# A long convolution and a feed-forward layer: earlier loads, a transform stage in 64-by-64 parts, products on a third engine, and a new deal of the tasks

## The chip, the cores and the metric

The kernel runs on one core of a Trainium2 chip. A core has five engines, each with its own queue of instructions that it issues in order: TensorE (PE; its weight loads are shown apart as PEld), VectorE (DVE), ScalarE (ACT), GpSimd (POOL) and SyncE (SP), which here issues nearly all DMA transfers. The metric is the time of one execution on the device, in microseconds (us).

## The reference, cut to what matters

```
x = A_u                                            # (1, 2048, 640)
mod = (silu(c) @ w_mod).reshape(1, 6, 1, -1)       # sa, ca, ga, sb, cb, gb
h = layernorm(x) * (1 + ca) + sa
  # A_ref(h): a convolution over the whole length L = 2048, per channel
  dt = exp(log_dt); A = -exp(log_A_real) + 1j * A_imag; C = (C_real + 1j * C_imag) * dt
  P = exp((A * dt)[:, :, None] * arange(L));  K = 2 * einsum("dn,dnl->dl", C, P).real
  y = irfft(rfft(h, 2 * L) * rfft(K, 2 * L))[:L]
x = x + ga * (y + h * D_skip)
h = layernorm(x) * (1 + cb) + sb
x = x + gb * ((silu(h @ w1) * (h @ w3)) @ w2)      # 640 -> 1728 -> 640
```

There are 640 channels, 128 states per channel, 2048 tokens.

## The kernel before, in words

The program has two parts. The **convolution** works in five blocks of 128 channels, counted 0 to 4 here. A token has the number 64 t1 + 16 q + j (t1 below 32, q below 4, j below 16), and the transforms of length 4096 are split in two stages along such numbers. For each block:

- *Generation* of the convolution's own kernel K, in eight chunks of 16 channels (`gen_chunk`): GpSimd makes phases (`ph<-p,p`) and sizes (`yy<-e,e`), ScalarE five sines (`tr<-ph`), VectorE five products (`yy<-yy,tr`, `xx<-tr,xx`), PE sums over the states in 32 matmuls (`kps<-yy,xx`), ScalarE copies to `ks`, VectorE adds the skip term.
- *Tokens*: the block's columns are normalised (`hn`, `hb`), written to DRAM (`hs`) and read back as `xb`.
- *First transform stage* (`first_tasks`): eight groups for the tokens (`ps<-wk,xb`), eight for K (`ps<-wk,ks`). A group is 8 matmuls of 64 x 128 tiles into one PSUM bank, and one copy by ScalarE or VectorE to `sp`, which holds both spectra's halves. In fp32 each matmul shows as two rows. A K group takes columns of all chunks, so the stage needs all eight chunks of its block.
- *Second stage and product* (`spectra_tasks`), eight spectra w.0 to w.7: PE makes `fh` (tokens) and `fk` (K), ScalarE holds `fh` in `hq`, VectorE multiplies with four instructions: `fp<-fk,hq`, `fk<-fk,hq`, and two sums into `fp`.
- *Inverse*: one per pair of spectra, z.0 to z.3 (`fz<-fp,wz`), whose two banks ScalarE or VectorE copies to `zt`; SP stores them in DRAM (`zd`).

Then **the last inverse stage** (`inverse`, matmuls `iy`, table `wd`, 1 MB, half of it zeros) reads `zd` back (`low<-zd`), adds the tokens x2 and gathers the second layernorm's sums. Its first rows (`ir0`, `ir1`) already run at the end of the convolution with the first four blocks' channels; the last block's channels follow when its stores are done, after eight `awake` matmuls that keep PE busy. The **feed-forward part** has 14 tiles of weights; each is split in a high part (ScalarE, `wh`) and a low part (GpSimd or VectorE, `wl`). Raw tiles `wr` (and `w2r`) have two buffers each, so that a third load waits for the split of the first. The first two tiles, 0 and 13, are loaded and split at the end of the convolution: tasks fw (load), fa (high part), fs (low part).

What sets the order: `run` lists all tasks of the convolution in a `Plan`, each with its engine and the tasks that it needs. The text ORDER is a list of task numbers; `Plan.run` issues the tasks in just this order (a letter a, d or p at a number picks ScalarE, VectorE or GpSimd where there is a choice), and `InOrder` ties each instruction to the one before on its engine. So every instruction of the convolution has the line of that helper, L147, in the profile. The task `change`, after the last generation chunk, closes the pools of the generation (`gw`, `tbl`, `gp`) and opens those of the feed-forward part. In it stand the loads of the first tokens and of `wd`; fw0, fw1 and the loads of the first rows (iz0, iz1) need it. These loads have one more condition, `behind`: they also wait for the last PE instruction ahead of them in the text:

```
nc.sync.behind = nc.tensor.prev
self.load_x2(0)
nc.sync.dma_start(self.wd, self.t_wd)
nc.sync.behind = None
```

Of the kernel before, what the change touches and what calls it, by code (L numbers as in the profile page):

```python
# [25 lines left out]
NB = 5  # L26
# [4 lines left out]
WA = 2  # L31
SIGN = -2 ** 31
# [11 lines left out]
284 294 285 298 352 148 458 299 445 149 0 582 698d 446 300 447 442 353d 592 324 699 443 450 328 325d 461 583d 336 459 460 329d  # L44
577 584 334 444 451 337a 585 301 972p 335a 700d 586 326 462 452 302 330 434 578d 327a 331a 354 448 467 593a 332 437p 579 438
468 439 580 333a 435 856 594 338 355a 453 449 436 358 463 581 595 851 464 475 440 364 454 469 465 455 339d 596 466 470 356 456
476 479 457 362 471 357 477 484 480 472 363 359 492 481 485 360 473 482 365 495 496 361 366 478 379 487 493 380 486 494 367
483 501 497 373 701 488 852a 375 502 857d 489 374 509 498 381 853 587 490 858 499 510 854 513 1399 859 390 704p 504 705 706
391 860 503 855 511 491 474 518 500 376 514 702 505 515 526 377 506 382 378 507 512 383 588a 407 519 527 384 520 528 408 385
861 589 516 703 508 530 590 517 521 591 368 529 707 388a 386a 522 389 543 531 387 536 523 532 537 1400d 369a 392 544 597 524  # L50
862a 545 525 393 1140 535 546 371a 394 533 1401 398 547 372 395 534 1402 1130 560 539 396 553 413 552 397 538 708 414 1403 370
399 540 548 863 564 400 549 561 864 565 554 709 865 598 541 566 569 710 542 401 550 599d 608 1131a 562 555 602 563 570 609a
1132 711p 606 973 712 571 713 604 1133 603d 714 1134 612 607d 1141d 600 601d 866 605a 974p 1142 567 610 613d 1246p 1404 1143
409 611d 551 572 670 568 1144 715 410 867a 636 573 411 574 732 556 719 1135 637 868 557 575 412 671 736 869 630 718 558 1405d
870 720 664 716 721 653 726 717 631 1409 1406 665 647 733 654 725 1407 871 648 734 741 1136a 415 681 724 735 1408 742 616 559
416 737 1414 1137 617a 743 738 417 682 1138 739 418 1139 687 722 744 1410a 620 727 880 723 1411 1125 688 728 749 881a 618 1412
740 576 1413 1415d 621a 729 766 753 876 619a 754 745 1126a 872 1416 750 1417 746 752 873d 1418 877a 1127 624 770 767 760 755
614 1128 768 625a 775 1129 628 615a 758 751 776 626 629a 769 759 622 627d 771 975 882 756 623d 772 761 402 883a 777 773 976
978d 730 778 979 419 774 980 403a 779 747 977 404 757 405d 632 420a 731 748 406 762 783 981 421 649 633 634 780 650 800 787
638 635 781 788 782 651 422a 763 639 789 423 652 655 784 764 640 790 884 656 801 641 878 885a 802 657 792 874 879a 785 658 765  # L60
786 875a 793 642 795 804 803 794 886 645a 643d 791 646 666 810 644 887a 817 1145 796 805 910 667 806 811 797 911 809 921 668
807 820 669 821 938 818 922 812 808 904 819 798 813 822 672 799 905 826 834 823 827 814 673 939 927 828 824 835 674 815 659
# [35 lines left out]
def shape_tables():  # L98
# [22 lines left out]
    wd = np.zeros((2, 32, 2, NJ, 2, 2, 32))  # L121
# [64 lines left out]
class K:  # L186
# [385 lines left out]
    def inverse_half(self, i, ps, tag, bufs):  # L572

        u, h = 2 + i // 2, i % 2
        if h == 0:
            self.zu = self.inverse_load(4608 + u % 2 * 2560, 2 * u, 2, 0, D)
# [1206 lines left out]
```

## Time and profile before

| | us |
|---|---|
| median of 3 runs | 968.23 (967.66 to 969.07) |
| the profiled execution | 967.95 |
| its span in the trace | 966.0 |
| PE busy in the span | 856.0 (89%) |
| VectorE busy | 713.6 (74%) |
| ScalarE busy | 518.4 (54%) |
| GpSimd busy | 336.2 (35%) |
| first matmul of the last inverse stage on the last block | 388.43 after the span's start |

The profiled execution is one among those timed; the span is what the trace shows from the first to the last instruction, and the remaining 1.95 us lie around it. A row such as `fk<-sp,wb 128*64 128x128 f32 x16` names output and inputs, the tile of PE, partitions by elements of the output, type and count. A bracket at a row's end is idle time of that engine before the row, and what ended it.

### The profile page before, as it was taken

What the parts mean: (1) busy time and instruction counts of PE and PEld (TensorE: products, weight loads), DVE (VectorE), ACT (ScalarE), POOL (GpSimd) and SP (SyncE); (2) the same over time, 40 slices, a digit from 0 to 9 for tenths busy, and PEclk for the clock granted to TensorE, in tenths of its full rate; (3) what the DMA queues carried; (4) which work ended last, traced back from release to release, by engine and by line L of the source; (5) the groups of instructions that cost most, each with busy time, mean ns of one, the idle gap of its engine ahead of it and who ended that gap; (6) DMA issues with size and microseconds to landing.
All of it is one profiled execution on the core that took longest, in us unless ns stands there. A gap on an engine that the chain in (4) does not pass through costs nothing.

```text
span 966.0 us, 20403 instructions
## 1 busy us (share of the span) xinstructions
PE 856.0 (89%) x8145; PEld 681.2 (71%) x8145; DVE 713.6 (74%) x1292; ACT 518.4 (54%) x874; POOL 336.2 (35%) x345
## 2 busy tenths in 40 slices
PE   2164867899999996899999999999999999999997
PEld 1033755787878772577787778888888888888875
DVE  7888899999999974565666486566468777765763
ACT  5889879979888840442343244344234444445331
POOL 2799898599999730100000000000113222300000
PEclk9597889999999997999999999999999999999999
DMA  9955426624040277875545263233031111123242
GB/s 245 253 172 209 106 61 168 162 70 111 25 111 25 69 224 230 200 202 150 158 121 137 82 157 103 82 85 106 28 82 55 55 55 55 42 82 92 86 150 82
DMA packets 124934, 113.20 MB, mean 117 GB/s; under 512 B 12328, under 2 KB 107048, under 8 KB 123432
## 3 DMA queue, kind: packets, MB, share of 16 engines
q1 hardware_dynamic: 124072, 110.99, 42.4%
q8 instruction: 64, 1.05, 0.5%
q10 hardware_dynamic: 768, 0.92, 0.4%
q14 instruction: 30, 0.25, 0.1%
HBM read 90.91 MB, written 20.97 MB: 116 GB/s over the span
## 4 chain that ended last, share of the span: by engine, by line
PE 57%; DVE 2%; DMA 2%; ACT 1%; issue 0%; SPq 0%; DVEq 0%; ACTq 0%
PE p L789 17%; PE acc L1036 16%; PE gu L999 7%; PE gu L1001 6%; PE gu L1000 6%; DMA wq<-in_w 1%; PE iy L562 1%; PE awake L147 1%; PE q L789 1%; PE tp L613 1%; PE fz L147 1%; DMA zd<-zt 0%; PE acc L147 0%; DVE w2l L988 0%; PE iy L147 0%; DVE wq L983 0%
## 5 line engine op out<-in xcount | busy, mean ns | idle before, releaser
L999 PE MATMUL gu<-xh,wh 128*128 128x512 f32 x270 | 106.0, 398 | 0.9 <-ACT xh L581 0.7
L1001 PE MATMUL gu<-xh,wl 128*128 128x512 f32 x270 | 105.4, 390 | 0.0
L1000 PE MATMUL gu<-xl,wh 128*128 128x512 f32 x270 | 105.2, 390 | 0.0
L789 PE MATMUL p<-x,wch 128*128 128x512 f32 x312 | 92.6, 390 | 0.0
L808 POOL TENSOR_TENSOR ws<-wp 128x256 f32<-128x256 f32 x13 | 9.6, 740 | 230.9 <-DVE x L582 116.0
L147 POOL TENSOR_TENSOR yy<-e,e 128x512 f32<-128x512 f32 x80 | 86.0, 1089 | 4.8 <-PE kps L147 3.6
L147 POOL TENSOR_TENSOR ph<-p,p 128x1024 int32<-128x1024 int32 x40 | 78.0, 1953 | 16.4 <-ACT tr L147 16.0
L147 DVE TENSOR_TENSOR yy<-yy,tr 128x512 f32<-128x512 f32 (+1 forms) x80 | 75.3, 946 | 1.6 <-POOL yy L147 1.2
L147 PE MATMUL kps<-yy,xx 128*32 128x64 f32 x2560 | 51.3, 235 | 23.2 <-DVE xx L147 12.9
L693 ACT ACTIVATE wh<-wr 128x640 fp32r<-128x640 f32 x51 | 34.9, 731 | 68.2 <-PE gu L1000 61.1
L147 PEld LDWEIGHTS kps<-yy,xx 128*32 128x32 f32 x2560 | 45.0, 117 | 34.0 <-issue 16.2
L789 PEld LDWEIGHTS p<-x,wch 128*128 128x128 f32 x312 | 58.3, 188 | 12.5 <-ACT s L824 0.4
L999 PEld LDWEIGHTS gu<-xh,wh 128*128 128x128 f32 x270 | 50.6, 188 | 16.8 <-issue 2.1
L1001 PEld LDWEIGHTS gu<-xh,wl 128*128 128x128 f32 x270 | 50.7, 188 | 11.3 <-DVE wl L702 0.4
L1000 PEld LDWEIGHTS gu<-xl,wh 128*128 128x128 f32 x270 | 50.7, 188 | 10.2 <-DVE xl L582 0.2
L789 PE MATMUL p<-x,wcl 128*128 128x512 f32 x156 | 57.0, 389 | 0.0
L147 ACT ACTIVATE tr<-ph,hpi 128x512 f32<-128x512 f32 x80 | 54.5, 689 | 3.0 <-DVE yy L147 2.1
L147 DVE TENSOR_TENSOR xx<-tr,xx 128x512 f32<-128x512 f32 x80 | 54.4, 682 | 1.7 <-ACT tr L147 1.5
L705 POOL MEMSET w2l<- 64x640 f32 x1 | 0.6, 632 | 157.0 <-PE acc L1036 157.0
L826 DVE TENSOR_TENSOR s<-p,s 128x512 f32<-128x512 f32 x52 | 34.8, 683 | 26.8 <-ACT s L824 22.8
L147 PE MATMUL ps<-wk,xb 128*64 128x128 f32 x640 | 46.8, 297 | 5.3 <-DVE hb L147 2.5
L1014 DVE TENSOR_TENSOR a<-a,gu 128x512 f32<-128x512 f32 x26 | 17.9, 687 | 45.5 <-PE gu L1001 45.4
(368 smaller groups left out, 2299.3 us busy)
## 6 DMA issues: line engine op xcount, KB each, us to landing
wr<-in_w SPq DMA_DIRECT2D x52, 320.0 KB, 3.6
zd<-zt SPq DMA_DIRECT2D x39, 256.0 KB, 2.7
w2r<-in_w SPq DMA_DIRECT2D x26, 320.0 KB, 3.0
wp<-in_w SPq DMA_DIRECT2D x26, 320.0 KB, 3.6
wq<-in_w SPq DMA_DIRECT2D x26, 320.0 KB, 3.2
low<-zd SPq DMA_DIRECT2D x48, 160.0 KB, 5.4
xs<-in_x SPq DMA_DIRECT2D x16, 320.0 KB, 9.8
hs<-hb SPq DMA_DIRECT2D x20, 256.0 KB, 2.7
```

The source lines that it names most:

```text
L147: self.prev = self.k.order(f(*a, **kw), self.prev)
L562: mm = nc.tensor.matmul(py[p][c:c + 32, :n], self.wd[r:r + 64, j0 + j + p, q // 2, c % 64:c % 64 + 32], z[q // 2][r:r + 64, j + p, o:o + n ...
L613: nc.tensor.transpose(pt[:, j * P:(j + 1) * P], xn[:, j, k * P:(k + 1) * P], self.ident)
L693: self.nc.scalar.activation(wh[:, i], raw[:, i], AF.Copy)
L789: nc.tensor.matmul(to, t[:, o], y[:, k], start=start and k == i == 0, stop=stop and (k, i) == (n - 1, 2), skip_group_check=True)
L808: G.tensor_tensor(s[0], a21, a22, op=ALU.add)
L826: add = lambda o, bk, s: V.tensor_tensor(o, bk, s, op=ALU.add)
L999: nc.tensor.matmul(pg, wh[:, k, :], xh[:, k, :], start=(k == 0), stop=False)
L1000: nc.tensor.matmul(pg, wh[:, k, :], xl[:, k, :], start=False, stop=False)
L1001: nc.tensor.matmul(pg, wl[:, k, :], xh[:, k, :], start=False, stop=(k == KT - 1))
L1014: nc.vector.tensor_mul(a, a, gu[1])
L1036: nc.tensor.matmul(acc[k], *two(a, w), start=(m == 0 and i == 0), stop=(m == 12 and i == 2))
```

## The change

**Memory.** Two pools are opened at the start and live to the end: `wrp` (two `wr`, two `w2r`; during the convolution they hold the tables pB, pS, al and mag) and `xp` (one tile of 3584 columns: first the tables of the odd blocks' sizes, then the first tokens with `wd`, then a part of the pair data of the feed-forward part). `wd` is stored without its zeros, 0.5 MB instead of 1 MB. The first rows' loads iz0 go to `xb`. `low` shrinks from 11264 to 7680 columns. Small early tiles lie in slices of the tile for layernorm sums.

**Loads.** fx (first tokens and `wd`), fw0, fw1 and iz0 no longer need `change`, and `behind` is gone there. They stand earlier in SP's order: fx among the stores of block 2, fw0 behind them, fw1 among the stores of block 3.

**K's first stage** in blocks 1 to 4 (`kernel_tasks`): four groups instead of eight; a group needs two chunks only, and consists of 32 matmuls of 64 x 64 tiles with 64 moving columns, into two banks, each with its own copy.

**Products.** In block 4 the spectra named in APART, w.2 and w.5, are multiplied by GpSimd: ScalarE copies `fk` to `sp` (SBUF) first, and GpSimd runs the four instructions on that copy.

**ORDER** is new from block 1 on. VectorE has 29 copies `sp<-ps` in it before, 21 after, and 10 copies `zt<-fz` before, 3 after; ScalarE has what VectorE lost.

```
 WA = 2
+APART = (2, 5)
...
+class Slices:
+    def __init__(self, t):
+        self.t, self.n = t.rearrange("p a b c -> p (a b c)"), 0
+    def tile(self, shape, ty, name):
+        self.n += shape[1]
+        v = self.t[:, self.n - shape[1]:self.n]
+        return v.bitcast(ty) if ty != F32 else v
...
     def first_tasks(self, b, m):
+        if m and b:
+            return self.kernel_tasks(b)
...
+    def kernel_tasks(self, b):
+        def mm(i):
+            for h in range(2):
+                pk[i, h] = self.pbank(f"ps{b}1{i}{h}")
+            for e in range(8):
+                x = self.ks[b][:, 8 * i + e, :]
+                for r in range(2):
+                    for h in range(2):
+                        g = slice(64 * h, 64 * h + 64)
+                        o = pk[i, h][r * 64:(r + 1) * 64].rearrange("p (v j i f) -> p i j v f", j=2, i=8, f=2)[:, e]
+                        nc.tensor.matmul(o, x[g], self.wk[g, r, g], start=True, stop=True, tile_position=(64 * h, 64 * r))
+        for i in range(4):
+            add(n + "m", "PE", 1.15, lambda i=i: mm(i), [f"g{b}.{2 * i}.d", f"g{b}.{2 * i + 1}.d"] + [f"w{b - 1}.{x}.k" for x in range(8)], ...)
+            for h in range(2):
+                add(n + f"e{h}", ("ACT", "DVE"), (.48, .61), lambda e, i=i, h=h: out(i, h, e), [n + "m"], ...)
...
+        def keep(i):
+            t = held[i, "k"] = four(self.sp[:, 0, 2 * i:2 * i + 2].rearrange("p v d f -> p (v d f)"))
+            nc.scalar.activation(t, bank.pop((1, i)), AF.Copy)
-            nc.vector.tensor_mul(to, k, bc(held[i][:, :, r], 2, 2))
+            self.eng(e).tensor_tensor(to, k, bc(held[i][:, :, r], 2, 2), op=ALU.mult)
...
+            apart = b == NB - 1 and i in APART
+            if apart:
+                add(n + "kk", "ACT", .52, lambda i=i: keep(i), [n + "k", n + "f"], t - q, give=[("bank", n + "k")])
...
-        add("fx", "SP", 0, None, ["change"], 0, dma=[327680] * 4 + [1048576])
+        add("fx", "SP", 0, load_tokens, [f"g{c}.{x}.z{i}" for c in (1, 3) for x in range(8) for i in range(3)] + ...
-            add(f"fw{m}", "SP", 0, lambda m=m: load_w(m), ["change"] + ([f"k{b}.{m}.m"] if m else []), W + 5, dma=[327680] * 3)
+            add(f"fw{m}", "SP", 0, lambda m=m: load_w(m), [f"t{b}.{h}.{i}" for h in range(2) for i in range(6)] + ...
-            q.behind = nc.tensor.prev
-            split[m] = self.weights_load(0, self.ORDER[m], self.wp, True)
-            q.behind = None
+            split[m] = self.weights_load(0, self.ORDER[m], None, True)
```

The first place is PE at the end of block 4's generation. Before:

```order
L147 MATMUL fk_4693<-sp,wb 64x128 x8
L147 MATMUL kps<-yy_4497,xx_4496 32x64 x32
L147 MATMUL fk_4746<-sp,wb 64x128 x8
L147 MATMUL kps<-yy_4582,xx_4581 32x64 x32
L147 MATMUL ps_4795<-wk,ks_4156 64x4x16x2 x8
L147 MATMUL ps_4806<-wk,ks_4156 64x4x16x2 x8
...
L147 MATMUL fh_4917<-sp,wb 64x128 x8
L147 MATMUL fk_4933<-sp,wb 64x128 x8
L147 MATMUL fk_4943<-sp,wb 64x128 x8
```

The rows left out are six more K groups and one inverse. After the change:

```order
L148 MATMUL ps_5011<-wk,ks_4390 64x2x16x2
L148 MATMUL ps_5012<-wk,ks_4390 64x2x16x2
L148 MATMUL kps<-yy_4764,xx_4763 32x64 x32
L148 MATMUL kps<-yy_4863,xx_4862 32x64 x32
L148 MATMUL ps_5123<-wk,ks_4390 64x2x16x2
L148 MATMUL ps_5124<-wk,ks_4390 64x2x16x2
...
L148 MATMUL fh_5157<-sp,wb 64x128 x8
L148 MATMUL fk_5192<-sp,wb 64x128 x8
L148 MATMUL fk_5204<-sp,wb 64x128 x8
```

Before, all K groups (ps) stand behind the last chunk's sums (kps); after, only the last of four groups does, and the fh and fk rows of block 4 follow it directly.

The second place is SP's list from the first tokens' load to the last stores. Before (the load of `wd`, the first weights, the first rows' loads, the third weight tile):

```order
L147 DMA low<-in_t_wd 128x2048
L147 DMA wr_0_4860<-in_w 128x5x128 x2
L147 DMA w2r_0_4863<-in_w 128x640
L147 DMA zd<-zt_4891 128x4x128
...
L147 DMA low<-zd 64x512 x8
L677 DMA wr_1_5417<-in_w 128x5x128 x2
L147 DMA zd<-zt_5016 128x4x128
L682 DMA w2r_1_5420<-in_w 128x640
L147 DMA zd<-zt_5031 128x4x128
L147 DMA low<-zd 64x512 x8
```

After the change the first tokens, `wd` and the first two weight tiles stand among stores of blocks 2 and 3, and the first rows' loads ahead of block 4's stores:

```order
L148 DMA x_low<-in_x 32x2560 x4
L148 DMA x_low<-in_t_wd 128x1024
...
L148 DMA wr_0_4656<-in_w 128x5x128 x2
L148 DMA w2r_0_4659<-in_w 128x640
...
L148 DMA wr_13_4883<-in_w 128x5x64 x2
L148 DMA w2r_13_4886<-in_w 64x640 x2
...
L148 DMA xb<-zd 64x512 x8
L148 DMA low<-zd 64x512 x8
```

The end of the convolution's stores, before:

```order
L677 DMA wr_2_5507<-in_w 128x5x128 x2
L682 DMA w2r_2_5510<-in_w 128x640
L147 DMA zd<-zt_5145 128x4x128
L147 DMA zd<-ztl 128x4x128
L147 DMA zd<-zt_5169 128x4x128
L147 DMA zd<-zt_5172 128x4x128
L548 DMA low<-zd 64x2x128 x4
```

and after the change, from the same first rows' loads on:

```order
L148 DMA zd<-zt_5267 128x4x128
L148 DMA zd<-zt_5299 128x4x128
L148 DMA zd<-zt_5332 128x4x128
L693 DMA wr_1_5664<-in_w 128x5x128 x2
L698 DMA w2r_1_5667<-in_w 128x640
L148 DMA zd<-zt_5345 128x4x128
L148 DMA zd<-zt_5347 128x4x128
L693 DMA wr_2_5754<-in_w 128x5x128 x2
L698 DMA w2r_2_5757<-in_w 128x640
L148 DMA zd<-ztl 128x4x128
L148 DMA zd<-zt_5376 128x4x128
L564 DMA low<-zd 64x2x128 x4
```

Before, four stores stood behind the load of the third weight tile (wr_1), and four behind that of the fourth (wr_2); after, four stores stand ahead of both, two behind wr_1 and two behind wr_2.

The third place is GpSimd's last work in the convolution. Before it had only the split of the two weight tiles, tile 0 (wl_0) first:

```order
L147 TENSOR_TENSOR xx_4581<-e_115,e_116 128x512
L147 TENSOR_TENSOR yy_4582<-e_115,e_116 128x16x32
L147 TENSOR_TENSOR wl_0_5026<-wr_0_4860,wh_0_4998 128x640 x2
L147 TENSOR_TENSOR w2l_0_5027<-w2r_0_4863,w2h_0_4999 128x640
L147 TENSOR_TENSOR wl_13_5084<-wr_13_4927,wh_13_5066 128x640
L147 MEMSET w2l_13_5085 64x640
L147 TENSOR_TENSOR w2l_13_5085<-w2r_13_4930,w2h_13_5067 64x640
```

After the change it multiplies the two spectra (fp, and sp as scratch), and then splits tile 13 ahead of tile 0:

```order
L148 TENSOR_TENSOR fp_5260<-sp,hq 128x2x2x128
L148 TENSOR_TENSOR sp<-sp,hq 128x512
L148 TENSOR_TENSOR fp_5260<-fp_5260,sp 128x256 x2
L148 TENSOR_TENSOR fp_5295<-sp,hq 128x2x2x128
L148 TENSOR_TENSOR sp<-sp,hq 128x512
L148 TENSOR_TENSOR fp_5295<-fp_5295,sp 128x256 x2
L148 TENSOR_TENSOR wl_13_5355<-wr_13_4883,wh_13_5247 128x640
L148 MEMSET w2l_13_5356 64x640
L148 TENSOR_TENSOR w2l_13_5356<-w2r_13_4886,w2h_13_5248 64x640
L148 TENSOR_TENSOR wl_0_5360<-wr_0_4656,wh_0_5177 128x640 x2
L148 TENSOR_TENSOR w2l_0_5361<-w2r_0_4659,w2h_0_5178 128x640
```

The buffer that wr_1 takes is that of tile 0, which is now freed last.

More of the change, by code (lines that the diff above doesn't have):

```diff
@@ L88 @@
+1515 1517
 """
@@ L622, in pair_x @@
     def pair_x(self, i, p=slice(None)):
-        return [self.px[i][:, h, p] for h in range(2)]
+        return [self.px[i][h][:, p] for h in range(2)]
     def ln_pair(self, xh, xl, pool, ps):
@@ L697, in low @@
         def low(eng):
+            wp = self.wp
             wh, w2h = parts
@@ L792, in load @@
         def load(m):
-            r = raw[m] = wp.tile([P, 2, KT, P], F32, name=f"wp_{m}", tag="wr", bufs=2)
+            r = raw[m] = self.wrp.tile([P, 2, KT, P], F32, name=f"wp_{m}", tag="wr", bufs=2)
             for i, src in enumerate((self.w1, self.w3)):
```

212 lines of the change are left out of this document (119 added, 93 removed).

## The prediction

> **What bounds the kernel now.** I read the page's slices first, to divide the run, then busy time by stretch, then the timeline of the stretch in which all engines thin out.
>
> ```profile
> span 966.0 us, 20403 instructions
> PE   2164867899999996899999999999999999999997
> DVE  7888899999999974565666486566468777765763
> ```
>
> One slice is 24.15 us. From slice 17 (about 400 us) to the end PE is full: that is the feed-forward part, and the diff changes there only where buffers lie. Before it VectorE is full, from about 120 us to 336 us, and between 336 and 400 us neither is. So the change can act in two places: the dense stretch, and the passage from convolution to feed-forward. Up to about 126 us both programs issue the same work in the same order. The stretches below are cut at the last VectorE product of each block's kernel generation.
>
> ```profile
> core 0: us, PE busy (x) PEld busy (x) DVE busy (x) ACT busy (x) POOL busy (x), PEclk, DMA share, GB/s
> 126.20:173.20 47.00, 31.68 (x592) 26.02 (x590) 46.52 (x87) 39.48 (x69) 40.77 (x44) 0.93 0.49 123
> 173.20:236.20 63.00, 57.75 (x1226) 47.86 (x1224) 61.12 (x112) 53.74 (x96) 50.33 (x52) 1.00 0.46 118
> 236.20:288.00 51.80, 48.80 (x1068) 41.63 (x1066) 51.58 (x94) 45.55 (x79) 49.49 (x48) 1.00 0.27 67
> 288.00:311.00 23.00, 22.12 (x526) 19.78 (x524) 21.47 (x41) 20.24 (x36) 21.63 (x20) 1.00 0.10 29
> 311.00:336.00 25.00, 24.60 (x516) 19.71 (x513) 24.90 (x45) 22.50 (x40) 20.06 (x16) 1.00 0.20 54
> 336.00:350.00 14.00, 12.96 (x248) 11.03 (x244) 6.61 (x14) 4.73 (x9) 0.00 (x0) 1.00 0.75 204
> 350.00:365.00 15.00, 13.40 (x154) 9.29 (x150) 14.71 (x31) 5.37 (x8) 8.27 (x6) 1.00 0.81 233
> 365.00:384.00 19.00, 11.08 (x46) 3.93 (x47) 7.52 (x24) 2.28 (x4) 0.00 (x0) 0.73 0.84 248
> ```
>
> From 126.2 to 336 us (209.8 us) VectorE is busy 46.52+61.12+51.58+21.47+24.90 = 205.6 us, ScalarE 181.5, GpSimd 182.3, PE 185.0. VectorE sets the pace; from 236 us on PE is 96% busy, so it is next. After 336 us VectorE is busy 6.61 of 14 us, then 14.71 of 15, then 7.52 of 19: a fill, one burst, and waits.
>
> ```profile
> 335.31 0.68 DVE L147 TENSOR_TENSOR xx<-tr,xx 128x512 f32<-128x512 f32 x1
> 336.63 1.17 PE L147 MATMUL kps<-yy,xx 128*32 128x64 f32 x64
> 337.74 1.97 PE L147 MATMUL ps<-wk,ks 128*64 128x128 f32 x32
> 338.12 0.38 ACT L147 ACTIVATE ks<-kps 128x256 f32<-128x256 f32 x1 [1.96 <-DVE ks L147]
> 340.75 2.84 PE L147 MATMUL ps<-wk,ks 128*64 128x128 f32 x48 [1.04 <-DVE fp L147]
> 345.44 2.84 PE L147 MATMUL ps<-wk,ks 128*64 128x128 f32 x48
> 349.02 2.01 PE L147 MATMUL fk<-sp,wb 128*64 128x128 f32 x32
> 350.16 0.69 DVE L147 TENSOR_TENSOR fp<-fk,hq 128x512 f32<-128x512 f32 x1 [2.01 <-PE fk L147]
> 355.78 5.91 SPq L147 DMA_DIRECT2D low<-zd  x8
> 361.79 1.10 SPq L677 DMA_DIRECT2D wr<-in_w  x2
> 362.99 0.47 SPq L147 DMA_DIRECT2D zd<-zt  x1
> 367.22 0.60 ACT L147 ACTIVATE zt<-fz 128x512 f32<-128x512 f32 x1 [6.04 <-DMA zd<-zt]
> 369.95 0.69 DVE L147 TENSOR_TENSOR low<-iy,low 128x512 f32<-128x512 f32 x1 [4.55 <-PE iy L147]
> 373.39 5.49 PE L147 MATMUL fz<-fp,wz 64*128 64x512 f32 x16 [3.58 <-DVE fp L147]
> 379.57 1.68 SPq L147 DMA_DIRECT2D zd<-zt  x2
> 381.36 7.13 PE L147 MATMUL awake<-low,ident 128*128 128x512 f32 x16 [1.46 <-DVE low L147]
> 383.78 2.58 SPq L548 DMA_DIRECT2D low<-zd  x4
> 388.43 0.65 PE L562 MATMUL iy<-low 64*32 64x128 f32 x24
> ```
>
> The last product of the last generation ends at 336.0 us. Then come kps, ks, all eight K-stage groups (ps<-wk,ks, 128 rows) and their copies, and only at 350.16 the first spectral product: 14.2 us. VectorE's burst of eight products follows. At 355.78 SP spends 5.91 us on issuing eight loads, so a spectrum that was ready before is stored at 362.99 only, ScalarE gets its zt buffer back at 367.22 (6.04 us late), and PE, then VectorE, stand behind that. The last two inverses run at 5.49 us for 16 rows. The last store's issue ends at 379.57+1.68 = 381.25, and the last load of spectra starts at 383.78. From there to the first feed-forward matmuls the programs are alike.
>
> **Part 1, the dense stretch.** Prices:
>
> ```profile
> L147 DVE COPY sp<-ps 128x512 f32<-128x512 f32 x29 | 19.7, 683 | 1.4 <-PE ps L147 1.4
> L147 DVE TENSOR_TENSOR fk<-fk,hq 128x512 f32<-128x512 f32 x40 | 27.5, 690 | 0.0
> L147 DVE TENSOR_TENSOR fp<-fp,fk 128x256 f32<-128x256 f32 x80 | 29.6, 412 | 0.1
> L147 ACT ACTIVATE sp<-ps 128x512 f32<-128x512 f32 x51 | 29.8, 589 | 13.2 <-PE ps L147 13.1
> ```
>
> Ahead of that last product VectorE loses 12 copies from PSUM (7 sp, 5 zt) and gains seven product instructions of block 3 (blocks count from 0 to 4) that were behind it: 12 x 0.683 = 8.2 us less, 0.69 + 2 x 0.69 + 4 x 0.412 = 3.7 us more, so 4.5 us less. (A normalisation and a magnitude product also leave; I leave them out as reserve.) ScalarE gains 17 copies: 17 x 0.589 = 10.0 us, 191.5 in all, still below VectorE's 205.6 - 4.5 = 201.1. If VectorE's 4.2 us of idle time stay, the stretch is 4.5 us shorter. I take **4 us**. From above it is 10 (reserve and all idle time gone); from below it is a loss of 5, because ScalarE is a queue in order and the list moves copies ahead of sines, and a sine that is late stops GpSimd:
>
> ```profile
> POOL ph L147 <- ACT tr L147: 16.0, 7, 8.8
> ```
>
> The K stage in 64-by-64 parts does the same sums in 256 matmul rows of 64 columns per block instead of 128 rows of 128. No such row exists. The cheapest bound is kps, 1.17 us for 64 rows (18 ns); the dearest is ps itself, 2.84 us for 48 (59 ns), as if the parts did not overlap. The nearest in shape, split in rows and columns, is iy at 388.43: 0.65 us for 24 rows, 27 ns. I take 27: 256 x 27 ns = 6.9 us per block against 128 x 59 ns = 7.6 us. So PE gains nearly nothing in the dense stretch, which I count as zero; the gain is in when the work can be done, Part 2.
>
> **Part 2, the passage**, on the clock of the old trace. *First product.* The K stage now needs only two finished chunks per group, and the list puts three of four groups ahead of the end of generation. After ks (ends 338.50) one group is left: 0.3 us hand-over (as from kps, 337.80, to ks, 338.12), 64 x 27 ns = 1.7, copies 0.7, the fk group 1.0 (2.01 for two) and hand-overs: first product at about **342.5** instead of 350.16, 7.7 us earlier.
>
> *VectorE.* Its window 350:365 holds 14.71 us in 31 instructions, 0.475 each; one product is four, 1.9 us. Six products instead of eight are 11.4 us, 353.9; PE, which has to put two inverses (half of 16 rows each) between the fk groups, holds it up by some 4 us: about 358. The last inverse takes another 1.9 us, its copies 0.7: **360.6**.
>
> *GpSimd* multiplies the other two:
>
> ```profile
> L147 POOL TENSOR_TENSOR yy<-e,e 128x512 f32<-128x512 f32 x80 | 86.0, 1089 | 4.8 <-PE kps L147 3.6 <-DVE hn L147 0.6 <-POOL ph L147 0.6
> L808 POOL TENSOR_TENSOR ws<-wp 128x256 f32<-128x256 f32 x13 | 9.6, 740 | 230.9 <-DVE x L582 116.0
> L147 POOL TENSOR_TENSOR wl<-wr,wh 128x640 fp32r<-128x640 f32 x3 | 4.6, 1553 | 21.7 <-ACT wh L147 21.7
> L147 ACT ACTIVATE wh<-wr 128x640 fp32r<-128x640 f32 x3 | 2.2, 734 | 0.2
> ```
>
> 2 x 1.09 + 2 x 0.74 = 3.7 us each. The first needs ScalarE's keep copy, which stands behind the first weights' high parts (3 x 0.734 = 2.2 us), a hold copy and its own fk group: about 345.4 to 349.1. The second's copy stands behind the first inverse's two: about 351.7 to 355.4. Then GpSimd splits the two weight tiles, 8.27 us in the window 350:365: until 363.7; the part that frees the first raw tile ends one 1.55 us instruction earlier, 362.1.
>
> *SP.* In the new order the next tile's loads (wr_1, wr_2) stand ahead of the last four stores, and wr_1 takes the buffer that this split frees. So SP waits until 362.1 and then issues wr (1.10 for two), w2r after 363.7, two stores, wr, w2r, two stores, at about 0.5 each: the last store's issue ends at **368**. The stores that are ready at 360.6 wait for that. Against 381.25 this is **13.2 us** earlier. The rest of the passage follows the last store and is taken as unchanged, as is the feed-forward part.
>
> Moving the token and weight loads ahead costs SP nothing: the buffers (tables of blocks 1 and 3, pB, al) come free before 336 us, with SP idle. The smaller table of the last stage (0.5 for 1 MB) is hidden likewise. If that cover were gone the loads would stand where they do now, some 5.9 us of SP issue at 356.
>
> **Sum.** The profiled execution took 967.95 us (span 966.0 and 1.95 outside); 967.95 - 4 - 13.2 = **951 us**. The median of the runs, 968.23, is 0.3 above it, inside their spread.
>
> **Rivals.**
> *A. More comes through (945).* The dense stretch gives 6.9 us and the splits are done before the products need GpSimd, so SP isn't held. Then the waking matmuls bind: they start after VectorE's last sums, near 365, and last 7.13, so iy starts at 372.2 instead of 388.43, 16.2 us earlier: 967.95 - 6.9 - 16.2 = 944.9. For it: VectorE is 98% busy. Against: SP's order is fixed.
> *B. A row of another tile shape drains PE (958).*
>
> ```profile
> L147 PE MATMUL kps<-yy,xx 128*32 128x64 f32 x2560 | 51.3, 235 | 23.2 <-DVE xx L147 12.9
> ```
>
> 15 of the 16 new groups stand between groups of other shapes ahead of the end; two drains each at one kps row's own time make 30 x 0.235 = 7.1 us. On PE that is 96% busy: 967.95 - 4 + 7.1 - 13.2 = 958. Against it: the kps rows at 336.63 end at 337.80, and the ps rows, of another shape, are running from 337.74: no gap.
>
> [...]
>
> *C. ScalarE becomes the bound (962).* One wait more like the 8.8 us above, and 2 us lost behind the weights' copies: 967.95 - 4 + 8.8 - 13.2 + 2 = 961.6. For it: the list gives ScalarE 10 us in a stretch where GpSimd already waited 16 us for it.
> *D. The K stage is dearer, and the kernel slower (973).* At ps's own 59 ns per row a block costs 256 x 59 = 15.1 us, 7.5 more. In blocks 2 to 4, where PE is 96% busy, two whole K stages and three quarters of the last one's lie ahead of the end of generation: 2.75 x 7.5 = 20.6 us, and 2 more (64 x 32 ns) in the last group: 967.95 - 17.2 + 22.6 = 973.4. It decides from 17.2/(2.75 x 256) = 24 ns above my price, 51 ns. For it: nothing in the trace runs 64 by 64. Against: iy, split in rows too, overlaps.
> *E. The passage moves but the stretch before it gives it back (968).* Four 4-us waits of the kind in C: no change.
>
> **How the numbers follow.** My forecast 0.46, A 0.16, B 0.09, C 0.15, D 0.10, E 0.04. A tenth or two of C and B may end at no change. A measurement of this kernel tells 0.2%, 1.9 us, from no change. Faster: 0.86 (forecast, A, B, C); same 0.04; slower 0.10. The range 941 to 963 takes in A with its dense stretch at 10 us, B and C; outside it stay D, E and a little.
>
> **What would show it.** Right: the first fp<-fk of block 4 within 8 us of the last xx; the K groups near 1.7 us for 64 rows; SP's wr load just ahead of the last four stores, ended by GpSimd; the last store's issue 30 to 33 us after the last xx (now 45). Wrong: K groups over 3 us (D), gaps ahead of and behind each (B), GpSimd waits for ACT tr above 16 us in sum (C), or the last xx after 340 us (E). If the feed-forward part, 398 to 966 now, is not 568 us long, my cut was wrong.

## The result, and the profile after

The changed kernel takes 978.74 us (median of 4 runs, 977.85 to 980.56) against 968.01 (4 runs, 967.66 to 969.07): 1.0111 times as long, 95% interval 1.0094 to 1.0129. It is slower by 1.1%, where 951 us were forecast. One execution among those below (1703.16 us, in the second run of experiment 1) was disturbed and is left out of its ratio. The page's slices of the changed kernel, its profiled execution:

```profile
span 978.8 us, 21433 instructions
PE   2164858688887988899999999999999999999997
DVE  7898888879887986455766585567377777765753
```

To see where the time is, I cut both traces at the same events: the last of each 16 products `xx<-tr,xx` (a block's generation has 16), the end of the last store's issue, the first row `iy` of the last stage on block 4, the first matmul of the feed-forward part. Lengths in us, worked out from the two timelines:

| stretch | before | after | difference |
|---|---|---|---|
| up to the end of block 0 | 103.8 | 104.0 | +0.2 |
| block 1 | 71.4 | 80.7 | +9.3 |
| block 2 | 61.7 | 67.9 | +6.2 |
| block 3 | 51.6 | 52.4 | +0.8 |
| block 4 | 47.6 | 54.6 | +7.0 |
| last product of generation to last store | 45.2 | 29.1 | -16.1 |
| last store to first `iy` | 7.2 | 7.4 | +0.2 |
| first `iy` to feed-forward | 9.6 | 13.4 | +3.8 |
| feed-forward to the end | 567.9 | 569.3 | +1.4 |

So the passage gained more than forecast (16.1 instead of 13.2), and the dense stretch, which was to give 4 us, took 23.3. The busy time by stretch of the changed kernel, cut at its own blocks' ends and at the last store:

```profile
core 0: us, PE busy (x) PEld busy (x) DVE busy (x) ACT busy (x) POOL busy (x), PEclk, DMA share, GB/s
126.20:184.60 58.40, 42.20 (x746) 35.30 (x748) 48.95 (x89) 43.90 (x85) 41.26 (x44) 0.85 0.43 113
184.60:252.60 68.00, 56.01 (x1308) 45.49 (x1306) 56.77 (x105) 61.38 (x104) 53.68 (x56) 0.92 0.39 97
252.60:305.00 52.40, 47.55 (x1248) 39.85 (x1248) 47.44 (x86) 44.31 (x79) 46.86 (x44) 1.00 0.30 73
305.00:359.60 54.60, 48.13 (x1236) 38.53 (x1226) 47.20 (x86) 42.56 (x75) 41.08 (x39) 0.94 0.41 110
359.60:388.70 29.10, 25.01 (x355) 16.31 (x356) 18.95 (x47) 10.89 (x20) 16.11 (x14) 0.98 0.64 176
```

From 126.2 to 359.6 us VectorE is busy 48.95 + 56.77 + 47.44 + 47.20 = 200.4 us, 5.2 less than the 205.6 of before: the work did leave it as counted. But the stretch is 233.4 us long, so VectorE stands idle 33.0 us in it, where it was 4.2. The granted clock is also below 1 in three of the four blocks (before: in the first alone), and in block 2 ScalarE is busy 61.38 of 68.00 us, more than any other engine. Three places in the timeline show how that comes about.

**Block 1: a wait in written order.** The changed kernel's timeline; a bracket is idle time ahead of the row and what ended it:

```profile
133.93 3.67 PE L148 MATMUL kps<-yy,xx 128*32 128x64 f32 x128 [8.47 <-DVE xx L148]
137.52 4.49 PE L148 MATMUL fh<-sp,wb 128*64 128x128 f32 x64
144.57 1.55 ACT L148 ACTIVATE hq<-fh 128x512 f32<-128x512 f32 x3
152.07 1.95 ACT L148 ACTIVATE hn<-xq,rs_n_h,rs_y_h 128x128 f32<-128x128 f32 x4 [1.69 <-DVE fp L148]
160.03 1.95 POOL L148 TENSOR_TENSOR ph<-p,p 128x1024 int32<-128x1024 int32 x1 [13.70 <-ACT tr L148]
```

PE waits 8.47 us for the sums of chunks 2 and 3 (kps), with four groups fh of block 0's spectra behind them in its list. ScalarE then has their holds, and normalised tokens, ahead of the sine that frees GpSimd's phase buffer, and GpSimd stands for 13.70 us.

**Block 4: an engine stops, and the profile shows no wait.** The same timeline around the early load of the first tokens and of `wd`, and the DMA queues of the stretch 300 to 320 us behind it:

```profile
302.19 1.89 SPq L148 DMA_DIRECT2D x_low<-in_x  x4
304.12 0.42 SPq L148 DMA_DIRECT2D x_low<-in_t_wd  x1
307.74 1.03 PE L148 MATMUL ps<-wk,xb 128*64 128x128 f32 x11
313.14 2.63 PE L148 MATMUL ps<-wk,xb 128*64 128x128 f32 x21 [4.37 <-issue]
315.81 0.69 DVE L148 COPY sp<-ps 128x512 f32<-128x512 f32 x1 [5.12 <-PE ps L148]
317.62 1.94 PE L148 MATMUL kps<-yy,xx 128*32 128x64 f32 x64
319.77 1.06 POOL L148 TENSOR_TENSOR yy<-e,e 128x512 f32<-128x512 f32 x1 [7.50 <-issue]
```

```profile
q1 hardware_dynamic: 864, 2.10, 41.9%
q8 instruction: 4, 0.07, 1.3%
```

PE stops after 11 of the 32 rows of one piece of work and goes on 4.37 us later; "issue" says that the profile shows no semaphore that held it. VectorE waits 5.12 us for PE's rows. GpSimd's 7.50 us bear "issue" as well, but they are a wait for PE: its sequencer waits there for semaphores of VectorE and PE, PE raises its own with the end of the sums kps (317.62 + 1.94 = 319.56 us), and GpSimd goes on at 319.77. So its stop follows from PE's. Four packets of instructions (q8), 0.07 MB, arrive in this stretch, among 2.10 MB of data.

**The passage**, of the changed kernel:

```profile
362.30 1.16 PE L148 MATMUL ps<-wk,ks 64*64 64x64 f32 x64 [1.44 <-DVE ks L148]
365.56 0.69 DVE L148 TENSOR_TENSOR fp<-fk,hq 128x512 f32<-128x512 f32 x1 [1.32 <-PE fk L148]
368.07 1.29 POOL L148 TENSOR_TENSOR fp<-sp,hq 128x512 f32<-128x512 f32 x1 [13.23 <-ACT sp L148]
376.96 1.42 POOL L148 TENSOR_TENSOR fp<-fp,sp 128x256 f32<-128x256 f32 x2
378.33 1.54 POOL L148 TENSOR_TENSOR wl<-wr,wh 128x640 fp32r<-128x640 f32 x1
379.01 1.40 DVE L148 TENSOR_TENSOR fp<-fp,fk 128x256 f32<-128x256 f32 x4
379.90 0.94 SPq L693 DMA_DIRECT2D wr<-in_w  x2
382.13 3.04 POOL L148 TENSOR_TENSOR wl<-wr,wh 128x640 fp32r<-128x640 f32 x2
385.19 1.86 SPq L693 DMA_DIRECT2D wr<-in_w  x2
388.19 0.46 SPq L148 DMA_DIRECT2D zd<-zt  x1
393.71 2.58 SPq L564 DMA_DIRECT2D low<-zd  x4
404.72 4.06 PE L629 MATMUL tp<-ident,xn 128*128 128x128 f32 x20 [2.65 <-ACT xn L613]
```

The last product of generation ends at 359.55. A K group of 64 rows takes 1.16 us, 18 ns a row. The first spectral product starts 6.0 us after generation, VectorE's last sum ends 20.9 after it, GpSimd's last 18.8 after it. Both loads `wr` stand among the last stores as in the list, and the last store's issue ends at 388.65. The load of its spectra starts 5.1 us later (before: 2.5).

Two statements ahead of the prediction are not so. The first is that wr_1 takes the buffer of tile 0: its load starts at 379.90, when GpSimd's split of tile 13 (`wl` x1) ends at 379.87, and the load of wr_2 starts at 385.19, when the split of tile 0 (`wl` x2) ends at 385.17. So wr_1 takes the buffer of tile 13. The second is that a K group of the old form needs all eight chunks. In the kernel before, three K groups of block 3 ran ahead of that block's last sums:

```profile
287.08 2.84 PE L147 MATMUL ps<-wk,ks 128*64 128x128 f32 x48
289.85 1.17 PE L147 MATMUL kps<-yy,xx 128*32 128x64 f32 x64
```

In its list of tasks a K group needs one chunk of its block and the eight `fk` groups of the block before. So the order of the list, and not the form of the groups, decides how early block 4's K stage can begin.

### The profile page after: what moved, and what is told of

Its sections match the earlier page's. It is cut to its first block, busy times and chain, and to the rows that moved or that the text cites. A ratio compares the mean times of both kernels' runs of the same rounds, so it can differ in the third digit from the quotient of the medians.

```text
span 978.8 us, 21433 instructions
## 1 busy us (share of the span) xinstructions
PE 858.0 (88%) x8657; PEld 679.3 (69%) x8657; DVE 700.1 (72%) x1262; ACT 527.5 (54%) x895; POOL 345.0 (35%) x356
## 4 chain that ended last, share of the span: by engine, by line
PE 64%; DVE 9%; ACT 9%; DMA 7%; issue 5%; POOL 4%; SPq 1%; ACTq 0%; DVEq 0%; POOLq 0%
PE p L807 16%; PE acc L1054 16%; PE gu L1017 7%; PE gu L1019 6%; PE gu L1018 6%; PE ps L148 4%; DMA xs<-in_x 2%; PE kps L148 2%; ACT tr L148 2%; DVE yy L148 2%; PE fk L148 2%; ACT hn L148 1%; DMA wq<-in_w 1%; DMA sp<-in_w_mod 1%; DVE xx L148 1%
## 5 line engine op out<-in xcount | busy, mean ns | idle before, releaser
L148 PE MATMUL kps<-yy,xx 128*32 128x64 f32 x2560 | 52.4, 239 | 31.6 <-DVE xx L148 17.8
L807 PE MATMUL p<-x,wch 128*128 128x512 f32 x208 | 68.4, 390 | 0.0
L148 PE MATMUL ps<-wk,xb 128*64 128x128 f32 x640 | 49.2, 305 | 9.8 <-issue 4.4
L148 POOL TENSOR_TENSOR yy<-e,e 128x512 f32<-128x512 f32 x48 | 52.4, 1106 | 10.2 <-issue 7.5
L148 PEld LDWEIGHTS ps<-wk,xb 128*64 128x64 f32 x640 | 44.5, 221 | 13.5 <-issue 5.5
L1030 ACT ACTIVATE th<-gu 128x512 f32<-128x512 f32 x26 | 15.5, 597 | 67.0 <-PE gu L1019 67.0
```

The lines of the kernel that those rows point to most:

```text
L148: self.prev = self.k.order(f(*a, **kw), self.prev)
L807: nc.tensor.matmul(to, t[:, o], y[:, k], start=start and k == i == 0, stop=stop and (k, i) == (n - 1, 2), skip_group_check=True)
L1030: nc.scalar.activation(th, gu[0], AF.Tanh, scale=0.5)
```

## The experiments

Each run's ratio is that to the kernel before on the same chip; the changed kernel has 1.0111. The list below names the two orders "old list" and "new list"; a task that exists only in the changed kernel (a K group of 64 by 64 parts) stands at the place of the old group that it replaces.

**1. Is it the list, and where?** Two runs take the old list up to a point and the new one behind it.

```
-ORDER: the new list
+ORDER: the old list up to the first K group of block 1; the remaining tasks in the new list's order
```

> The old list of tasks up to the first K group of block 1, the new one behind it. In the changed kernel the last product of block 1's generation ends 10.7 us later than before (184.6 against 173.9 us). Theory 'list' (the new deal makes the engines wait for each other in their written order, each place by itself): block 1 ends near 174 again and the whole takes 967 to 970. Rival 'given back' (a later engine is the limit, so that a block that ends sooner only waits longer): 976 to 979. Rivals 'K stage' (the 64 by 64 groups stall PE and the PSUM banks) and 'loads' (the early loads hold SP or collide with something): nothing of theirs stands before block 1's end, so what they cost stays, and they too would give 967 to 970.

Measured: 971.08 us, ratio 1.0034 (1.0015 to 1.0053). Block 1 is 72.6 us long (old 71.4, changed 80.7), block 2 is 69.9, blocks 3 and 4 52.9 and 53.7, much as in the changed kernel. That is 1.1 us above the range of "list" and well below that of "given back". The loss of block 1 belongs to its own list; of the 8.1 us won there, block 2 gives back 2.0.

```
-ORDER: the new list
+ORDER: the old list up to the first K group of block 3; the remaining tasks in the new list's order
```

> The old list up to the first K group of block 3, with the new 64 by 64 K groups of blocks 1 and 2 at the old groups' places; the new list from there. Changed kernel: VectorE idles 9.5, 11.2, 5.0 and 7.4 us in blocks 1 to 4, before 0.5, 1.9, 0.2 and 1.6. 'List': blocks 1 and 2 and part of 3 return to the old idle times, 18 to 22 us less: 957 to 961. 'K stage': block 1 returns, but blocks 2 and 3, whose K groups are the new ones, keep their idle time: 966 to 970. 'Given back': 974 to 979.

Measured: 964.57, ratio 0.9969 (0.9958 to 0.9981), some 4 us above the range of "list" and below those of the rivals. Blocks 1 to 4 are 70.7, 61.9, 52.9 and 55.8 us long. So block 2's 8.0 us between these two runs are the list's as well, with the new K groups in both. That fits the stretch table: the new list gives ScalarE 61.38 us of work in block 2, the old one 52.6 (61.9 less 9.3 of idle time in this run). But ScalarE is idle for 6.6 us of the changed kernel's block 2, so that its work alone is the limit there isn't shown. Nor is it block 1's wait again, as the waits of that block say (columns: in total, times, longest):

```profile
POOL ph L148 <- ACT tr L148: 6.8, 4, 2.4
PE ps L148 <- ACT hq L148: 4.9, 2, 3.7
```

Before, GpSimd waited 10.4 us for a sine in block 2, and PE 0.6 for ScalarE's holds. Which tasks of block 2 cost most stays open.

**2. A single piece of block 1's list.**

```
+w0.3.f w0.3.h  w0.2.f w0.2.h  w0.7.f w0.7.h  w0.4.f w0.4.h  w0.5.f w0.5.h   among the sines of chunk 3
 g1.3.p g1.2.p
-w0.3.f w0.7.f w0.4.f w0.2.f w0.5.f, and their holds (h) behind them
```

> The changed kernel with one small piece of its list moved, in block 1: the five groups fh of block 0's spectra 3, 2, 7, 4, 5 and ScalarE's holds of them stand among the sines of chunk 3, where the old list has the first of them, instead of behind the sums (kps) of chunks 2 and 3. In the changed kernel PE stands still for 8.5 us ahead of these sums, and GpSimd later for 13.7 us, because ScalarE has these holds and four normalisations ahead of the sines that free GpSimd's buffer. 'Holds' (that one place makes most of block 1's loss of 10.7 us): block 1 ends at 176 to 179 instead of 184.6, the whole takes 970 to 974. Rival 'normalisations' (the waits come from the normalised tokens, whose loads and products stand early in the new list): block 1 ends at 182 or later, 976 to 979.

Measured: 972.96, ratio 1.0074 (1.0045 to 1.0102). Block 1 ends at 179.07 us, 5.6 earlier; 1.6 of that is block 0's, where the list is the same, so that block 1 itself is 76.7 us long, 4.0 less. Three of that run's waits from 126 to 180 us (columns as above):

```profile
POOL ph L147 <- ACT tr L147: 11.0, 3, 9.8
ACT hn L147 <- DMA xq<-in_x: 6.1, 3, 2.6
PE kps L147 <- DVE xx L147: 3.3, 3, 2.7
```

PE's wait falls from 8.5 to 3.3 us, GpSimd's longest only from 13.7 to 9.8: ten tasks of 1518 make 4.0 of the block's loss of 9.3 us, somewhat under half. The normalised tokens, for whose loads ScalarE now waits 6.1 us (2.0 in the changed kernel), may be a part of the rest; that is not shown. The time lies in the range of "holds", but the block's end does not: this place is not most of the loss.

**3. The old list up to the end of generation.**

```
-ORDER: the new list
+ORDER: the old list up to the end of block 4's generation (K groups of block 4 and all loads behind it); the rest in the new order
```

> The old list up to the end of block 4's generation, the new K groups at the old groups' places (block 4's all behind the generation), first tokens and weights loaded behind the change of pools; only the rest of the new list, with two products on GpSimd. 'List': the generation ends at 336 us as before or a little sooner, and the end gains 3 us from the shorter K stage (4 groups of 1.16 us against 7.6) and some from the two products, 4 to 8 us in all: 960 to 964. 'K stage': the generation ends 10 us or more later than 336 and the time is 970 or more. 'Loads': 955 to 964, like 'list', since the loads stand late.

Measured: 973.41, ratio 1.0062 (1.0042 to 1.0082). "K stage" has such a time, but with a generation that ends 10 us late; it ends at 338.99 us, 3.0 late. So none of the three fits. Blocks 1 to 4 are 71.5, 62.0, 53.8 and 49.0 us: 4.0 us longer than before together, so the new K groups at the old places, with all else that this run keeps of the change, cost about 1 us per block, not 10. What is lost is the passage: 45.0 us, as long as before, though the K stage is shorter and GpSimd makes two products; and 10.9 us from the last store to `iy` instead of 7.2. So the passage's gain hangs on K groups and loads ahead of the end of generation. This run moves both back and can't part them; the next one moves the first tokens' load alone and loses 6.2 us of passage.

**4. The early load.** First it goes back behind the change of pools:

```
-... z2.2.o1 fx ...            (x_low<-in_x x4, x_low<-in_t_wd)
+... change fx fa0 ...
```

> Only the load of the first tokens and the last stage's table moved: from behind block 2's stores to behind the change of pools. In the changed kernel PE stands still for 4.4 us in the midst of a group of matmuls at 308.8 us, and GpSimd for 7.5 us at 312.3, both with no releaser, just behind this load of 1.8 MB at 302 us. 'Loads': these two stops are gone, block 4's generation ends 5 to 7 us sooner, and the whole takes 972 to 975 (a part is paid at the end, where the load now stands). 'List': the stops are not from the load, the time is 978 to 982.

Measured: 977.47, ratio 1.0100 (1.0072 to 1.0128). It lies between the ranges of "loads" and "list". Block 4 is 49.2 us long instead of 54.6, as "loads" has it, but the passage is 35.3 instead of 29.1: what was won is paid there. The timeline of this run:

```profile
352.96 2.32 SPq L147 DMA_DIRECT2D x_low<-in_x  x4
358.03 0.68 PE L147 MATMUL ps<-wk,ks 64*64 64x64 f32 x26 [1.44 <-DVE ks L147]
362.98 1.34 PE L147 MATMUL ps<-wk,ks 64*64 64x64 f32 x38 [4.27 <-issue]
```

The stop has gone along with the load: it begins 5.7 us after the load's issue (6.6 in the changed kernel), now in the midst of a K group, and is 4.27 us long; GpSimd's is gone. Then the load stays early, but in pieces:

```
-self.load_x2(0)                       # four loads
-nc.sync.dma_start(self.wd, self.t_wd)
+# five tasks fx0, fx1, fx2, fx3, fx, 20 list places apart; each but the first:
+nc.sync.behind = nc.tensor.prev       # the load also waits for the last PE instruction in the list
+nc.sync.dma_start(...)                # one of the five
+nc.sync.behind = None
```

> The changed kernel, its load of the first tokens and of the last stage's table cut in its five transfers, each behind a PE instruction some 4 us after the one before; nothing else moved. 'Loads in one go' (1.8 MB at once keep PE's and GpSimd's next instructions waiting): PE's stop of 4.4 us and GpSimd's of 7.5 us in block 4 are gone or below 2 us, block 4 ends 4 to 6 us sooner, and as the loads still stand ahead of the end, all of it comes through: 972 to 975. 'List': the stops stay, 978 or more.

Measured: 972.56, ratio 1.0064 (1.0041 to 1.0087). The same piece of PE work in this run's timeline, and GpSimd's:

```profile
306.58 1.64 PE L147 MATMUL ps<-wk,xb 128*64 128x128 f32 x21 [1.14 <-issue]
310.79 1.07 POOL L147 TENSOR_TENSOR yy<-e,e 128x512 f32<-128x512 f32 x1 [1.83 <-issue]
```

4.37 and 7.50 us have become 1.14 and 1.83, and GpSimd again goes on just after PE's sums end (310.65). Block 4 is 49.1 us long, 5.5 less, the passage 29.0 as in the changed kernel. Nothing was moved but the same 1.8 MB, so this loss is the load in one go.

**5. The stores, and the waking matmuls.**

```
+if not ahead and self.last_load is not None:
+    self.order(i, self.last_load)     # each later weight load behind the last low<-zd of the last stage
```

> The changed kernel with one thing moved: the loads of the third and fourth weight tile (wr_1, wr_2) stand behind the loads of the last block's spectra instead of among the last four stores. In the changed kernel the last store's issue ends at 388.65 us, the load of these spectra begins at 393.71, the first matmul of the last stage on it starts at 396.04, when the waking matmuls end (387.14 + 8.83), and the feed-forward part's first matmul comes 13.4 us later (before: 9.6). Theory 'stores held' (the two loads hold the stores, then share the transfer with them and with the loads behind): last store's issue near 384, its landing and the next load faster by 2.5 us too, but the waking matmuls still end at 396, so only the 13.4 us shrink to about 10: 974.5 to 976.5. Rival 'not held': the stores end where they do, 977.5 to 979.5. Rival 'weights late': the feed-forward part waits for its third tile: 980 or more.

Measured: 975.23, ratio 1.0067 (1.0042 to 1.0093). The passage is 24.9 us instead of 29.1, the feed-forward part begins 10.0 us after the first `iy` instead of 13.4; in between the waking matmuls hold the start, as expected (10.1 us from store to `iy`). Then four of them instead of eight:

```
-self.awake(nc.tensor, po.tile([P, 512], F32, name="awake0", tag="acc4"), 8)
+self.awake(nc.tensor, po.tile([P, 512], F32, name="awake0", tag="acc4"), 4)
```

> As the last one, and four waking matmuls instead of eight ahead of the last stage. 'Waking binds' (with the stores out of the way the eight waking matmuls set the start of the last stage): the last stage starts near 391.5 instead of 396, the whole takes 970 to 972. Rival 'the load binds': it starts when the spectra have landed, 394 or later, 973.5 to 976. Rival 'clock': PE falls to a lower granted clock and what is gained is lost in the turns (tp) and first products: the same as the last one or slower.

Measured: 974.07, ratio 1.0054 (1.0034 to 1.0074). `iy` starts at 390.56 instead of 393.93, but the feed-forward part comes 12.9 us behind it. Two rows of the timeline and one of the stretches of this run:

```profile
390.56 1.84 PE L581 MATMUL iy<-low,x_low 64*32 64x128 f32 x20
399.36 3.88 PE L633 MATMUL tp<-ident,xn 128*128 128x128 f32 x20 [2.73 <-ACT xn L617]
```

```profile
400.00:403.50 3.50, 3.30 (x18) 2.90 (x15) 1.70 (x3) 1.61 (x4) 0.00 (x0) 0.51 1.03 222
```

The 32 rows `iy` last from 390.56 to 393.85, 3.3 us instead of 1.4: at a granted clock of 1.00 they wait for the load `low<-zd`, so "the load binds" has the larger part. The granted clock is 0.51 in the turns, and the 20 of them take 3.88 us instead of 2.40, of which 0.8 come back in the wait behind them; that is "clock". 2.9 of the 3.4 us are lost again. That fewer waking matmuls make the clock fall isn't shown. The run of experiment 6 has eight, and its turns are as slow:

```profile
405.51 3.98 PE L632 MATMUL tp<-ident,xn 128*128 128x128 f32 x20 [2.48 <-ACT xn L616]
```

**6. The two products on GpSimd**, on top of the stores put first:

```
-APART = (2, 5)
+APART = ()
```

> Compared with the run with stores first (975.2): the two products that GpSimd makes of block 4's spectra 2 and 5 are made by VectorE again, without ScalarE's copies of them; nothing else differs. 'Products on the path' (the prediction's sum: one product is 1.9 us of VectorE): 2 to 4 us slower, 977 to 979. Rival 'PE and copies bind' (VectorE has that time free, it idles between its products in the passage): 974 to 976. Rival 'GpSimd is in the way' (its products delay its splits of the weights): faster, 971 to 974.

Measured: 982.92, ratio 1.0166 (1.0138 to 1.0194); the run with stores first has 1.0067. That is above all three ranges. The passage is 31.7 us instead of 24.9. PE's rows, and VectorE's sums of two products:

```profile
367.87 1.09 PE L147 MATMUL fz<-fp,wz 64*128 64x512 f32 x2 [0.26 <-DVE fp L147]
370.16 1.41 DVE L147 TENSOR_TENSOR fp<-fp,fk 128x256 f32<-128x256 f32 x4
371.06 3.58 PE L147 MATMUL fz<-fp,wz 64*128 64x512 f32 x6 [2.10 <-DVE fp L147]
374.57 3.66 PE L147 MATMUL fk<-sp,wb 128*64 128x128 f32 x32
```

PE stops inside one inverse of 8 rows for 2.10 us. The row names VectorE's sums as what ended the stop, and the times agree: the second of the four ends at 370.91, and PE goes on at 371.06. So this is a wait for VectorE, and not a stop like that of block 4. Then PE runs at about half speed: 3.58 us for 6 rows, 3.66 for 32, where the run with stores first has 2.21 for 8 and 2.04 for 32; the granted clock is 0.53 from 371.0 to 378.3. VectorE in turn waits 5.08 us for PE. So the two products are on the path, as the first theory has it, and cost 6.8 us of passage, more than the 3.8 of VectorE's own time. The lower clock follows their stop; what they would cost at the full clock isn't shown. Another 2.0 us stand between `iy` and the feed-forward part.

**7. Together.** The old list up to block 3's K groups, the new one behind it, stores first, four waking matmuls:

```
-ORDER: the new list
+ORDER: as in the second run of 1
+self.order(i, self.last_load); awake0: 4
```

> The old list up to the first K group of block 3 (as in the second run, 964.6), the new list behind it, stores first, four waking matmuls. If what the parts cost adds up: 964.6 less 3 for the stores and 3 to 5 for the waking matmuls, 956 to 959. If the end is bound by the load of the spectra instead: 960 to 963.

Measured: 960.13 us, ratio 0.9911 (0.9881 to 0.9942): faster than the changed kernel, and than the one before by 0.9%. The time lies where an end bound by the load of the spectra was expected (960 to 963), above the sum of the parts (956 to 959). Then with the load in five pieces, and with the two weight loads also held until the last stage's matmuls:

```
+fx0, fx1, fx2, fx3, fx, each behind a PE instruction
```

> As the last one, with the load of the first tokens and of the last stage's table cut in its five transfers, each behind a PE instruction some 4 us after the one before, instead of 1.8 MB in one go. In the second run PE stood still for 2.1 us at 295 us and GpSimd for 4.1 us behind it, just after this load, and VectorE idled 5.9 us in block 4. 'Loads' (a transfer of 1.8 MB in one go keeps PE's and GpSimd's next instructions waiting): these stops are gone, 2 to 4 us less than the last one. 'List' (the stops have another reason): within 1 us of it, with the same stop.

Measured: 960.41, ratio 0.9919 (0.9896 to 0.9942). PE's stop in block 4 falls from 1.91 us to 0.43, the block from 55.3 to 52.9 and the passage from 27.5 to 24.6; but the time is the same. In the profiled executions, 957.1 and 956.2 us of span, block 0 is longer by 1.0 us, block 1 by 0.9, the start of the last stage by 0.9 and the feed-forward part by 1.9 (570.0 against 568.1). The gain is there in the convolution's end and not in the whole; why not, the runs don't tell.

```
+if m in (1, 2) and b == 0:
+    self.held_back(i)                 # wait for the last stage's matmuls on block 4
```

> As the combined kernel with the spread load (960.4), but the loads of the third and fourth weight tile also wait for the last stage's matmuls on the last block, so that they no longer share the transfer with the spectra. In that run the last stage's 32 rows took from 374.26 to 377.1 and the feed-forward part began 11.9 us after its first row. 'Shared transfer': 1.5 to 2 us less, 957.5 to 959.5. Rival 'weights late': the third tile is waited for, 961 or more.

Measured: 961.00, ratio 0.9945 (0.9924 to 0.9967): no gain. The time is that of "weights late", but PE's waits show none for the third tile. The rows `iy` last 2.5 us instead of 2.9, the turns 4.07 instead of 3.33, and the feed-forward part comes 12.4 us after `iy` instead of 11.9: a shared transfer is not what makes these 12 us. The number of waking matmuls doesn't sort the runs either: it is 10.0 us (stores first) and 12.0 (experiment 6) with eight, 11.9 to 12.9 with four. What makes them stays open.

## Why the prediction was wrong, step by step

- **"If VectorE's 4.2 us of idle time stay, the stretch is 4.5 us shorter": this is the step that failed.** The work fell by 5.2 us as counted; the idle time went from 4.2 to 33.0. The sum took a list that no trace had run, kept the old list's idle time for it, and bounded it from below with a loss of 5 us. The two list runs put 16 us of it on the lists of blocks 1 and 2; the spread load puts 5.5 us on block 4's load.
- **Rival C had the mechanism and a wrong size.** It named ScalarE's fixed order, a late sine and a GpSimd that stands behind it, at 8.8 us once. Its sign, more than 16 us of such waits in sum, came:

```profile
POOL ph L148 <- ACT tr L148: 24.8, 11, 13.7
```

13.7 us of them are block 1's. In block 2 this wait fell. The counterpart "191.5 in all, still below VectorE's" summed over four blocks, and the sum hid that ScalarE is fullest in block 2, with 61.38 busy us against VectorE's 56.77. E (no change) counted four such waits of 4 us; from 4 us won to 23.3 lost it would have needed seven. Its sign, a last `xx` after 340 us, came as well (359.55).
- **"Moving the token and weight loads ahead costs SP nothing" was true, and the wrong question.** The price is on PE, a stop of 4.37 us, and on GpSimd, which waits for PE's sums behind it: 5.5 us of block 4. Before, a load of the same tokens and a table twice as large at 339.79 stopped no engine visibly.
- **The K stage's price:** 27 ns a row were taken; 18 ns were measured, the lower bound. D (59 ns) falls. In the third experiment, with the new groups at the old places, a block is still about 1 us longer.
- **B (a drain at each change of shape) falls.** The trace doesn't show the two drains of 0.235 us per group that its sum counts. At 22 of the 26 places of the changed kernel where a K group meets rows of another shape PE has no gap; three gaps end with work of ScalarE or VectorE, and one, of 2.02 us at 198.65, bears "issue". In the rows below, the sums end at 349.40 + 1.15 = 350.55, and the K group runs from 350.48, with no gap:

```profile
349.40 1.15 PE L148 MATMUL kps<-yy,xx 128*32 128x64 f32 x64 [0.97 <-DVE xx L148]
350.48 1.16 PE L148 MATMUL ps<-wk,ks 64*64 64x64 f32 x64
```

- **The passage was right in its times, and in part by luck.** Forecast from the last product of generation: first spectral product 6.5 us, VectorE's end 24.6, GpSimd's second product done 19.4, last store 32; measured 6.0, 23.6 (the last copy), 18.8 and 29.1. That the last stores wait behind the weight loads, and these for GpSimd, was right too, and putting them first gave 4.2 us of passage. Two reasons were wrong. "The K stage now needs only two finished chunks per group" is no gain, since an old group needed one; the list made the K stage early. And the sum let both loads wait for one split, until 26.1 us after generation; the trace has two waits, 20.4 and 25.6 us, since wr_1 follows tile 13, and the last store comes 3 us earlier than forecast.
- **"The rest of the passage follows the last store and is taken as unchanged":** off by 3.8 us between `iy` and the feed-forward part, where the load of spectra began 5.1 us after the store, the rows `iy` waited for it (0.22 and 0.20 us), and the turns ran at a lower granted clock (0.58 from 404.7 to 408.8 us, and 4.06 us long; before 1.00 from 394.9 to 397.4, and 2.41). Of the 1.4 us in the feed-forward part I have no cause.

## What to carry to other kernels

When a written order of tasks is replaced, counting what each engine has to do bounds the gain and says nothing of the waits; ask of every stretch which engine is fullest in that stretch, and for each long wait of the old trace what now stands ahead of the instruction that ended it. A list made of parts can be tested in parts: taking the old list up to a point tells each block's loss within a few runs, and kept what was good of the new one (960 us). A large load that is moved ahead of where it is needed should be looked at for what it meets there, on every engine and not only on its own queue. And an idle time that bears "issue" is not yet a stop without a cause: see first whether another engine's work ends just ahead of its end, as with GpSimd here.

## What the runs showed of the hardware

In these runs PE stopped in the midst of a group of matmuls, with no semaphore that the profile shows, after 1.8 MB of loads had been issued within 2.35 and 2.79 us: for 4.37 us in the changed kernel, 6.6 us after the first load's issue, and for 4.27, 5.7 us after it, when the load was moved. When the same load came in five pieces, the stop was 1.14 us long. In the changed kernel a packet of instructions of 16 KB landed at 311.84 us, 1.30 us before PE went on (313.14). That PE waits there for its next instructions, and that the data delay them, is my guess from these times and not shown; the runs show the stop, the packet and the dependence on the load.

In the changed kernel PE's rows were also slower just after the stop: 64 rows of a K group took 1.16 us in the passage, where the granted clock was 1.00 (362.30 to 363.46), and 1.99 us from 315.70 on, where it was 0.50:

```profile
314.00:316.00 2.00, 2.00 (x29) 1.67 (x29) 0.19 (x1) 1.87 (x3) 0.00 (x0) 0.50 0.03 8
315.70 1.99 PE L148 MATMUL ps<-wk,ks 64*64 64x64 f32 x64
```
